# One group of row sums in the last half, a last output block in two column halves, and a new order for every operation

## The chip, the core and the metric

The kernel runs on one core of a Trainium2 chip. TensorE (PE) multiplies matrices, VectorE (DVE), ScalarE (ACT) and GpSimd (POOL) work element by element, and SyncE (SP) issues the DMA transfers. Each engine has its own queue and works it off in order; semaphores make an engine wait for another. The metric is the device time of one execution in microseconds, as the median over several runs.

## What is computed

Two stages follow each other. The first is a retention: per batch and head a 64 x 64 state decays and gathers outer products, and each row of q is multiplied with it.

```python
for t in range(S):                       # S = 768, 4 batches, 8 heads, D = 64
    state = gamma * state + einsum('bhd,bhe->bhde', k[:, :, t], v[:, :, t])
    y[:, :, t] = scale * einsum('bhd,bhde->bhe', q[:, :, t], state)
```

The heads' outputs side by side are x, 4 batches of 768 rows with 512 columns. The second stage is a mixture of four attention experts: two experts are chosen per row by a gate, each has its own q, k, v and output weights with 64 inner columns, and the attention is causal.

```python
logits = x @ w_gate                      # the two largest of 4 experts per row, softmax over the two
for e in range(4):
    q, k, v = x @ wq[e], x @ wk[e], x @ wv[e]
    a = exp(causal(scale * q @ k.T) - max);  a /= a.sum(-1) + 1e-09
    out += w[:, e] * (a @ v @ wo[e])     # w is 0 where e is not chosen
```

## The kernel before

The 768 rows of each batch are two halves of 384 rows (`HS`), so there are eight half-sequences j = 0 to 7; each has three blocks (`CH` = 3) of 128 rows (`C`). The four experts are two pairs p, with two experts e in each.

Retention works on 24 chunks of 128 rows (6 in a batch), each as two steps of 64 rows. For each chunk SP loads `qkT_t` (L245) and `kv_t` (L249), 512 KB each; DVE (first chunk) or POOL multiplies decay factors in (L260 for k, L275 for q); `h2` (L380, L386) computes the part inside the steps and `h1` (L321, L325) the state and its product. ACT and DVE turn the result into `xh` and `xl`, a high and a low part, so that three matmuls in a reduced format replace one in full precision. The weights come in the same way: `wload` (L214) brings a piece into a buffer that is free at the start, ACT (L220) writes its high part and DVE (L221) its low part.

For each half j follow: `proj` (L436, q and k), `vgate` (L478, v and gate logits, per block), `gate` and `gate2` (the two weights per row; `wn` has them per row, `wt` transposed), `mpass` (L559, L573, row maxima on DVE), `mrow` (L602), `score` (L685, L686: transposed scores into `ps`, ACT's exponential L692 into `pt`, a causal select L698 on POOL for diagonal blocks, and additions of all `pt` of a pair into `ac`, L707 and L714, on DVE or POOL) and `av` (L731: `pt` times v, gathered in `ob`, 64 rows for each expert of the pair).

The rows' sums of exponentials divide the result. For j = 0 to 6 this is `norm_a` and `norm_b`: 12 matmuls (L754) of columns of `sel` with `ac` put the sums of all experts and blocks into one tile `f`; DVE adds 1e-9 (L760), takes reciprocals (L764) and multiplies with the expert weights `wt` (L765); SP writes `f` to DRAM (L768) and reads it back spread over partitions (`fe`, L772); POOL multiplies `on`, a copy of `ob`, with `fe` (L781), ACT rounds to `oh` (L783), and POOL subtracts to get `ol` (L786).

For the last half j = 7 there is `norm_last(j, p, c)`, six times, for each pair p and block c. It sums `ac` over partitions with two matmuls against `ones` (f1, L801), copies the block of `ob` with ACT (L806), makes the factors in `rw` in three small DVE steps (f2, L810 to L812), spreads them with two matmuls of `rw` against the identity into `fb` (f3, L818), multiplies on DVE (L822), rounds on ACT (L824) and subtracts on DVE (L827). `wout` (L845) then multiplies `oh` and `ol` with the output weights, three matmuls for each pair, six for each block; ACT evicts 128 x 512 (L853), and SP writes 256 KB (L855).

The order of the work is not that of the code. Each call of `op` records one operation: its engine, a function that emits its instructions, and what it reads and writes. `arrange(ORDER, SLOTS)` at the end emits them in the order of a literal table of operation numbers, and a second table names, for each kind of buffer, which of its few slots each new buffer takes. The framework puts the semaphores in.

## Time and profile before

| | us |
|---|---|
| median of 3 runs | 328.45 (327.85 to 329.1) |
| span of the profiled execution | 325.9 |
| time of that execution beside its span | taken for the median: 2.55 more |

| engine | busy us | share of the span |
|---|---|---|
| PE | 315.4 | 97% |
| DVE | 172.3 | 53% |
| POOL | 169.7 | 52% |
| ACT | 130.1 | 40% |

A profile row gives the start in us, the busy time in us, the engine, the line, the operation, what it writes and reads, the shape, and how many instructions are put together; brackets hold the idle time of the engine before it and what ended it. "x4" for a full-precision matmul of two halves counts the trace's own records, two for each matmul of the program. Matmuls overlap in the pipeline, so the time that one takes of TensorE is the distance to the next one's start, not its busy time.

### The profile page before, as it was taken

The numbers are of one execution on the slowest core, as the hardware profiler recorded it, in microseconds if no ns is written. First come the engines' busy times: TensorE is split into PE (matmuls) and PEld (weight loads), VectorE is DVE, ScalarE is ACT, GpSimd is POOL, SyncE is SP. The second block draws the span as 40 slices with busy tenths as digits, with TensorE's granted clock in tenths as the row PEclk, the third lists the DMA queues.
The fourth block names the chain that finished last, engine by engine and source line by source line (L and its number), as shares of the span: only waits on it lengthen the run. The fifth ranks groups of instructions, "written<-read, shape, count | busy, mean of one in ns | idle before, by whom it ended". The sixth has DMA issues, their size and how long they took to land.

```text
span 325.9 us, 11205 instructions
## 1 busy us (share of the span) xinstructions
PE 315.4 (97%) x4738; PEld 274.7 (84%) x4738; DVE 172.3 (53%) x478; ACT 130.1 (40%) x322; POOL 169.7 (52%) x189
## 2 busy tenths in 40 slices
PE   7599999999999999999999999999999999999995
PEld 3489998898988799979988799989879799887673
DVE  1654566665553354866352453856434234886842
ACT  1244212442734226422636224443433525437633
POOL 6665323561793967333398752671375731922800
PEclk9959999999999999999999999999999999999999
DMA  7994996434746627526646474374320503423022
GB/s 276 384 384 143 249 291 209 152 95 120 198 129 215 230 82 183 142 85 197 179 134 193 166 242 129 80 232 157 98 61 2 165 24 91 134 78 114 0 100 98
DMA packets 22072, 50.82 MB, mean 156 GB/s; under 512 B 3619, under 2 KB 8311, under 8 KB 22021
## 3 DMA queue, kind: packets, MB, share of 16 engines
q1 hardware_dynamic: 22020, 50.10, 49.8%
q8 instruction: 37, 0.61, 0.7%
q14 instruction: 15, 0.11, 0.1%
HBM read 30.71 MB, written 6.79 MB: 115 GB/s over the span
## 4 chain that ended last, share of the span: by engine, by line
PE 94%; DMA 3%; DVE 1%; issue 1%; ACT 1%; SPq 0%; ACTq 0%; DVEq 0%
PE ps L436 21%; PE ps L478 11%; PE ps L845 11%; PE ps_o L731 10%; PE ps L685 7%; PE ps L686 7%; PE ps_st L321 6%; PE ps L386 5%; PE ps L573 4%; PE ps L559 2%; PE ps L325 2%; PE ps L380 2%; PE ps L754 2%; DMA ot<-in_wvg_dram 2%; PE ps_st L731 1%; DMA am_t<-in_amask_dram 1%
## 5 line engine op out<-in xcount | busy, mean ns | idle before, releaser
L692 ACT ACTIVATE pt<-ps 128x384 f32<-128x384 f32 (+2 forms) x112 | 49.1, 493 | 15.8 <-PE ps L686 14.6
L581 DVE CUSTOM_DVE_ANT_0 scr<-ps,cmask_t 128x128 bf16<-128x128 f32 (+3 forms) x64 | 29.8, 487 | 35.3 <-PE ps L573 34.9
L698 POOL TENSOR_SCALAR_AFFINE_SELECT pt<-pt 128x256 f32<-128x256 f32 x48 | 20.9, 445 | 50.1 <-ACT pt L692 39.8
L436 PE MATMUL ps<-xh,qk_hi 128*128 128x384 f32 x128 | 44.0, 344 | 0.0
L685 PE MATMUL ps<-q,k 128*128 128x384 f32 (+2 forms) x144 | 43.9, 318 | 0.0
L436 PE MATMUL ps<-xh,qk_lo 128*128 128x384 f32 x128 | 43.2, 338 | 0.4 <-issue 0.4
L436 PE MATMUL ps<-xl,qk_hi 128*128 128x384 f32 x128 | 43.1, 336 | 0.0
L686 PE MATMUL ps<-q,k 65*128 65x384 f32 (+2 forms) x144 | 42.2, 313 | 0.0
L714 POOL TENSOR_TENSOR ac<-ac,pt 128x256 f32<-128x256 f32 (+2 forms) x32 | 39.9, 1248 | 1.9
L275 POOL TENSOR_TENSOR qd<-qkT_t,qdec_t 128x512 f32<-128x512 f32 (+1 forms) x23 | 27.9, 1212 | 24.7 <-issue 11.0
L707 POOL TENSOR_TENSOR ac<-pt,pt 128x512 f32<-128x512 f32 (+1 forms) x14 | 21.3, 1525 | 32.2 <-ACT pt L692 31.7
L731 PE MATMUL ps_o<-pt,vt 128*64 128x384 f32 (+2 forms) x252 | 35.5, 421 | 0.0
L441 ACT ACTIVATE k<-ps 128x384 fp32r<-128x384 f32 x32 | 15.7, 492 | 49.3 <-PE ps L436 49.3
L335 DVE TENSOR_TENSOR sblk<-ps_st,sdec_t 128x256 f32<-128x256 f32 x44 | 18.5, 421 | 29.7 <-PE ps_st L321 21.7
L348 ACT ACTIVATE xh<-ps 128x512 fp32r<-128x512 f32 x24 | 14.3, 597 | 45.4 <-PE ps L325 45.4
L321 PE MATMUL ps_st<-kv_t 64*64 64x64 f32 x704 | 30.0, 224 | 1.8 <-POOL kv_t L260 0.7
L380 PE MATMUL ps<-am,kv_t 64*64 64x64 f32 x768 | 27.8, 223 | 2.5 <-issue 2.3
L260 POOL TENSOR_TENSOR kv_t<-kv_t,kdec_t 128x512 f32<-128x512 f32 (+1 forms) x23 | 22.4, 977 | 14.8 <-DMA kv_t<-in_kv_dram 11.4
L321 PEld LDWEIGHTS ps_st<-kv_t 64*64 64x64 f32 x704 | 25.1, 137 | 5.9 <-issue 3.6
L731 PEld LDWEIGHTS ps_o<-pt,vt 128*64 128x64 f32 x252 | 16.6, 136 | 15.8 <-issue 11.7
L325 PE MATMUL ps<-qd,sblk 64*64 64x64 f32 x704 | 29.9, 224 | 0.0
L478 PE MATMUL ps<-vg_hi,xh 128*128 128x260 f32 x96 | 28.8, 300 | 0.0
(115 smaller groups left out, 781.5 us busy)
## 6 DMA issues: line engine op xcount, KB each, us to landing
kv_t<-in_kv_dram SPq DMA_DIRECT2D x24, 512.0 KB
qkT_t<-in_qkT_dram SPq DMA_DIRECT2D x24, 512.0 KB
out_dram<-ot SPq DMA_DIRECT2D x24, 256.0 KB
q<-k SPq DMA_DIRECT2D x28, 192.0 KB
k<-q SPq DMA_DIRECT2D x14, 192.0 KB
k<-k SPq DMA_DIRECT2D x14, 192.0 KB
fe<-fd SPq DMA_DIRECT2D x28, 96.0 KB
pt<-in_wqk_dram SPq DMA_DIRECT2D x4, 256.0 KB
```

The source lines that it names most:

```text
L321: nc.tensor.matmul(ST[b].t[rows(rt), s * D:(s + 1) * D], kvs(m, 0, s)[rows(rt)], kvs(m, 1, s)[rows(rt)], start=c == 0 and s == 0, stop=Fal ...
L325: nc.tensor.matmul(yo(m, rt, s), SB[m % 2][rows(rt), s], LD[g, 2].t[rows(rt), s, m % 2 * SC:(m % 2 + 1) * SC], start=m % 2 == 0 and s == 0 ...
L380: nc.tensor.matmul(yo(2 * g + u, rt, s), kvs(u + 2 * g, 1, s)[rows(rt)], amg.t[rows(rt), u, s], start=g % NC == 0 and u == 0 and s == 0, s ...
L436: nc.tensor.matmul(pb.t[:, :HS], ww[:, kt, wsl], xx[:, kt], start=n == 0, stop=n == 11)
L478: nc.tensor.matmul(pb.t[:, :NV + E], xx[:, kt, sl], ww[:, kt], start=n == 0, stop=n == 11)
L581: lambda: nc.vector.tensor_tensor_reduce(scr.t[:, :n1], pb.t[:, :n1], K["cmask"][:, HS + C - n1:], 1.0, mx0.t[:, e, i:i + 1] if prior else ...
L685: nc.tensor.matmul(o, k1.t[:, e, ko:ko + C], q1.t[:, e, q0:], start=True, stop=False)
L686: nc.tensor.matmul(o, k2.t[:65, e, ko:ko + C], q2.t[:65, e, q0:], start=False, stop=True)
L692: lambda es=es, sb=sb, n=n: nc.scalar.activation(pt.t[:, es[0]:es[0] + n, q0:], sb.t[:, :n * w].rearrange("p (e t) -> p e t", e=n), AF.Exp ...
L714: op(eng, cost, lambda: en.tensor_tensor(ac.t[:, :, q0:], ac.t[:, :, q0:], pt.t[:, :, q0:], op=OP.add), r=[(pt, 0), (pt, 1), (ac, "b")], w ...
L731: nc.tensor.matmul(ob.t[e * 64:e * 64 + 64, q0:HS], vt.t[:, ko // C, ee * 64:ee * 64 + 64], pt.t[:, e, q0:], start=kb == 0, stop=kb == las ...
L845: nc.tensor.matmul(wb.t, oo[:, sl], ww[:, p], start=n == 0 and p == 0, stop=n == 2 and p == NP - 1)
```

## The change

First, `norm_f(j)` is split off from `norm_a`: the sums and the three DVE steps that make `f`. The last half runs it once, for all pairs and blocks, so `ones`, `rw`, f1 and f2 go. Its f3 takes a column of the identity, spread to 64 columns, as the stationary operand and `f` as the moving one. ACT now copies `fb` to `on`, and DVE multiplies `ob` with that. The dependency of `ob` is kept per block of 128 columns, so a block is free to be read when its last `av` is through. Second, the last block of `wout` is done in two halves of 256 columns, each with its own `ps`, eviction (part 0 on ACT, part 1 on DVE) and DMA of 128 KB. Third, `stream_a` appends the last half's `norm_last` and `wout` units at its end. Fourth, ORDER and SLOTS are new from the first entry on, for 1549 operations instead of 1555. Line numbers shift by a few: L754 is now L753, L818 is L811, L845 is L842, L853 is L856, L855 is L858.

```diff
--- before.py
+++ after.py
@@ -176,7 +176,6 @@
-    RW = tag("rw", 2, [128, 2])
@@ -231,7 +230,6 @@
-    ones = sbuf.tile([128, 1], F32, name="ones")
@@ -731,20 +729,21 @@
                 nc.tensor.matmul(ob.t[e * 64:e * 64 + 64, q0:HS], vt.t[:, ko // C, ee * 64:ee * 64 + 64],
                                  pt.t[:, e, q0:], start=kb == 0, stop=kb == last, skip_group_check=True)
 
-        op("PE", 3.75 * (HS - q0) * COL, fn, r=[(vt, ko // C), (pt, 0), (pt, 1)], w=[(ob,)],
+        op("PE", 3.75 * (HS - q0) * COL, fn, r=[(vt, ko // C), (pt, 0), (pt, 1)],
+           w=[(ob, c) for c in range(q0 // C, CH)],
            new=[ob] if kb == 0 else [], mode="128x64")
         if kb == last and j < NJ - 1:
             on = ONB[j, p] = Buf(ON)
-            op("ACT", act_c(HS), lambda: nc.scalar.activation(on.t, ob.t[:, :HS], AF.Copy), r=[(ob,)], w=[(on,)],
+            op("ACT", act_c(HS), lambda: nc.scalar.activation(on.t, ob.t[:, :HS], AF.Copy),
+               r=[(ob, c) for c in range(CH)], w=[(on,)],
                new=[on])
 
     def actok(ac):
         return [(ac, "a"), (ac, "b")]
 
-    def norm_a(j):
+    def norm_f(j):
         DONE.add(("n", j))
-        sb, f, fd, fe, wt = Buf(PB), Buf(FF), Buf(FD), Buf(FE), WTB[j // 2]
-        FEB[j] = fe
+        sb, f, wt = Buf(PB), Buf(FF), WTB[j // 2]
         acs = [ACB[j, p] for p in range(NP)]
         c0 = j % 2 * CH
 
@@ -765,6 +764,14 @@
             nc.vector.tensor_tensor(f.t, f.t, wt.t, op=OP.mult)
 
         op("DVE", 1.3, f2, r=[(f,), (wt,)], w=[(f,)])
+        return f
+
+    FLAST = []
+
+    def norm_a(j):
+        f, fd, fe = norm_f(j), Buf(FD), Buf(FE)
+        FEB[j] = fe
+        c0 = j % 2 * CH
         op("SP", 0.4, lambda: nc.sync.dma_start(fd.t, f.t), r=[(f,)], w=[(fd,)], new=[fd], nbytes=65536)
         for e in range(E):
             def bc(e=e):
@@ -788,39 +795,28 @@
 
     def norm_last(j, p, c):
         sl = slice(c * C, c * C + C)
+        if not FLAST:
+            FLAST.append(norm_f(j))
         if c == 0:
             OS[j, p] = (Buf(OH), Buf(OL))
             ONB[j, p] = Buf(ON)
         oh, ol = OS[j, p]
-        on, ac, ob, wnb = ONB[j, p], ACB[j, p], OTB[j, p], WNB[j // 2]
+        on, ob, f = ONB[j, p], OTB[j, p], FLAST[0]
         fresh = c == 0
-        nb, fb, rw = Buf(PB), Buf(PB), Buf(RW)
-
-        def f1():
-            for e in range(2):
-                nc.tensor.matmul(nb.t[:, e:e + 1], ac.t[:, e, sl], ones, start=e == 0, stop=e == 1,
-                                 skip_group_check=True)
-
-        op("PE", 0.4, f1, r=actok(ac) + [("ones",)], w=[(nb,), (rw, "n")], new=[nb, rw],
-           mode="128x128")
-        op("ACT", act_c(C), lambda: nc.scalar.activation(on.t[:, sl], ob.t[:, sl], AF.Copy), r=[(ob,)],
-           w=[(on, c)], new=[on] if fresh else [])
-
-        def f2():
-            nc.vector.tensor_scalar(rw.t, nb.t[:, :2], 1e-9, None, op0=OP.add)
-            nc.vector.reciprocal(rw.t, rw.t)
-            nc.vector.tensor_tensor(rw.t, rw.t, wnb.t[:, 2 * p:2 * p + 2, CH + c], op=OP.mult)
-
-        op("DVE", 0.5, f2, r=[(nb,), (wnb,)], w=[(rw,)])
+        fb = Buf(PB)
 
         def f3():
             for e in range(2):
-                nc.tensor.matmul(fb.t[e * 64:e * 64 + 64, :C], rw.t[:, e:e + 1].to_broadcast([128, 64]), K["ident"],
+                r = (2 * p + e) * 32 + CH + c
+                nc.tensor.matmul(fb.t[e * 64:e * 64 + 64, :C], K["ident"][:, r:r + 1].to_broadcast([128, 64]), f.t,
                                  start=True, stop=True, skip_group_check=True)
 
-        op("PE", 0.24, f3, r=[(rw,), ("ident_t",)], w=[(fb,)], new=[fb], mode="128x64")
-        op("DVE", dve_c(C), lambda: nc.vector.tensor_tensor(on.t[:, sl], on.t[:, sl], fb.t[:, :C], op=OP.mult),
-           r=[(on, c), (fb,)], w=[(on, c)])
+        op("PE", 0.24, f3, r=[(f,), ("ident_t",)], w=[(fb,), (on, c, "n")], new=[fb] + ([on] if fresh else []),
+           mode="128x64")
+        op("ACT", act_c(C), lambda: nc.scalar.activation(on.t[:, sl], fb.t[:, :C], AF.Copy), r=[(fb,)],
+           w=[(on, c)])
+        op("DVE", dve_c(C), lambda: nc.vector.tensor_tensor(on.t[:, sl], ob.t[:, sl], on.t[:, sl], op=OP.mult),
+           r=[(on, c), (ob, c)], w=[(on, c)])
         op("ACT", act_c(C), lambda: nc.scalar.activation(oh.t[:, sl], on.t[:, sl], AF.Copy), r=[(on, c)], w=[(oh, c)],
            new=[oh] if fresh else [])
         op("DVE", dve_c(C),
@@ -829,31 +825,38 @@
 
     WP = {}
 
-    def wout(j, i, pairs=(0, 1)):
+    def wout(j, i, pairs=(0, 1), part=None):
         b, half = divmod(j, 2)
         hi, lo = W["wo"]
         first = pairs[0] == 0
+        n0, n1 = (0, Dm) if part is None else (part * 256, part * 256 + 256)
         if first:
-            WP[i] = Buf(PB)
-        wb = WP[i]
+            WP[i, part] = Buf(PB)
+        wb = WP[i, part]
         sl = slice(i * C, i * C + C)
         os = [OS[j, p] for p in pairs]
 
         def fn():
             for p, (oh, ol) in zip(pairs, os):
                 for n, (oo, ww) in enumerate(((oh.t, hi), (oh.t, lo), (ol.t, hi))):
-                    nc.tensor.matmul(wb.t, oo[:, sl], ww[:, p], start=n == 0 and p == 0, stop=n == 2 and p == NP - 1)
+                    nc.tensor.matmul(wb.t[:, :n1 - n0], oo[:, sl], ww[:, p, n0:n1], start=n == 0 and p == 0,
+                                     stop=n == 2 and p == NP - 1)
 
         last = pairs[-1] == NP - 1
         ot = Buf(OT) if last else None
-        op("PE", 3 * len(pairs) * 0.233, fn, r=[(x, i) for o in os for x in o] + wtok("wo"),
+        op("PE", 3 * len(pairs) * (n1 - n0) * 0.455e-3, fn, r=[(x, i) for o in os for x in o] + wtok("wo"),
            w=[(wb,)] + ([(ot, "n")] if last else []), new=[b for b, y in ((wb, first), (ot, last)) if y],
            mode="128x128")
         if last:
-            op("ACT", act_c(512), lambda: nc.scalar.activation(ot.t, wb.t, AF.Copy), r=[(wb,)], w=[(ot,)])
+            if part == 1:
+                op("DVE", dve_c(256), lambda: nc.vector.tensor_copy(ot.t[:, :256], wb.t[:, :256]), r=[(wb,)],
+                   w=[(ot,)])
+            else:
+                op("ACT", act_c(n1 - n0),
+                   lambda: nc.scalar.activation(ot.t[:, :n1 - n0], wb.t[:, :n1 - n0], AF.Copy), r=[(wb,)], w=[(ot,)])
             r0 = half * HS + i * C
-            op("SP", 0.4, lambda: nc.sync.dma_start(out[b, r0:r0 + C], ot.t), r=[(ot,)], w=[("out", j, i)],
-               nbytes=262144)
+            op("SP", 0.4, lambda: nc.sync.dma_start(out[b, r0:r0 + C, n0:n1], ot.t[:, :n1 - n0]), r=[(ot,)],
+               w=[("out", j, i, part)], nbytes=512 * (n1 - n0))
 
     def wouts(j):
         return [(COST["wout"], lambda i=i: wout(j, i)) for i in range(CH)]
@@ -876,10 +879,6 @@
                     u.append((4 * w(kb - 1) * COL, lambda p=p, kb=kb: av(j, p, kb - 1)))
                     if kb < nkb and kb >= 2 and wl:
                         u.append(wl.pop(0))
-                if j == NJ - 1 and kb > CH:
-                    i = kb - CH - 1
-                    u.append((COST["norm"] / 3, lambda p=p, i=i: norm_last(j, p, i)))
-                    u.append((COST["wout"] / 2, lambda p=p, i=i: wout(j, i, (p,))))
         if j:
             us[0].insert(1, (0, lambda: norm_b(j - 1), ("n", j - 1)))
         if j < NJ - 1:
@@ -891,7 +890,14 @@
             for k in range(NP):
                 u += us[k][:2]
                 us[k] = us[k][2:]
-        return u + wl
+        u += wl
+        for c in range(CH):
+            for p in range(NP):
+                u.append((COST["norm"] / 3, lambda p=p, c=c: norm_last(j, p, c)))
+            for x in range(2 if c == CH - 1 else 1):
+                for p in range(NP):
+                    u.append((COST["wout"] / 2, lambda p=p, c=c, x=x: wout(j, c, (p,), x if c == CH - 1 else None)))
+        return u
 
     def merge(lists, offs=(0, 0, 0)):
         tot = [sum(x[0] for x in l) + 1e-9 for l in lists]
@@ -926,7 +932,6 @@
-        op("DVE", 0.06, lambda: nc.vector.memset(ones, 1.0), w=[("ones",)])
@@ -1006,93 +1011,96 @@
 ORDER = (
...
-    3, 1, 2, 5, 6, 4, 7, 12, 8, 13, 9, 10, 14, 19, 20, 21, 99, 0, 23, 100, 101, 102, 103, 26, 1313, 24, 25, 22, 28,
...
+    0, 22, 3, 1, 23, 4, 25, 27, 5, 98, 28, 2, 24, 14, 56, 7, 6, 26, 9, 12, 13, 44, 58, 37, 39, 40, 38, 43, 48,
...
 SLOTS = {
...
-    "f": "0000000",
+    "f": "00000000",
-    "kv_t": "012012012012012012012012",
+    "kv_t": "012021020122101201010222",
-    "on": "0120120120120120",
-    "ot": "01210210102102102102102102",
+    "on": "0120102102120212",
+    "ot": "012010210122101200121200120",
-    "qd": "010101010101010101010101",
-    "qkT_t": "012012012012012012012012",
-    "rw": "010101",
+    "qd": "010101010101001011010100",
+    "qkT_t": "012012012020221020120120",
...
 }
```

Three places show how the tables move instructions. The first is SP's queue at the start of the program, which loads the chunks (`qkT_t`, `kv_t`), constants (`am_t`, `sdec_t`, `qdec_t`, `kdec_t`) and the v weights (`in_wvg_dram`). Before:

```order
L249 DMA kv_t_66<-in_kv_dram 128x1024
L245 DMA qkT_t_63<-in_qkT_dram 128x1024
L195 DMA am_t<-in_amask_dram 128x256
L195 DMA sdec_t<-in_sdec_dram 128x48
L195 DMA qdec_t<-in_qdec_dram 128x256
L195 DMA kdec_t<-in_kdec_dram 128x48
L245 DMA qkT_t_64<-in_qkT_dram 128x1024
L249 DMA kv_t_67<-in_kv_dram 128x1024
L214 DMA ot_127<-in_wvg_dram 128x260
L245 DMA qkT_t_65<-in_qkT_dram 128x1024
```

After:

```order
L247 DMA kv_t_66<-in_kv_dram 128x1024
L243 DMA qkT_t_63<-in_qkT_dram 128x1024
L194 DMA kdec_t<-in_kdec_dram 128x48
L194 DMA sdec_t<-in_sdec_dram 128x48
L194 DMA am_t<-in_amask_dram 128x256
L247 DMA kv_t_67<-in_kv_dram 128x1024
L243 DMA qkT_t_64<-in_qkT_dram 128x1024
L194 DMA qdec_t<-in_qdec_dram 128x256
L213 DMA ot_127<-in_wvg_dram 128x260
L247 DMA kv_t_68<-in_kv_dram 128x1024
```

The number behind a name is the buffer. `kv_t_67` takes chunk 1 before and chunk 2 after; chunk 1's load of `kv` was the second of its kind, ahead of the first weights, and is now the third (`kv_t_68`), behind the first weights. `qdec_t` stands later, `kdec_t` earlier. The second place is TensorE in the last half, where the last scores are through. `ps_o` and `ps_st` are the `ob` of the two pairs. Before:

```order
L818 MATMUL ps_145<-ident_t,rw_133 64x128 x2
L731 MATMUL ps_o_146<-pt_111,vt_94 64x128 x2
L731 MATMUL ps_st_147<-pt_112,vt_94 64x256 x2
L818 MATMUL ps_142<-ident_t,rw_134 64x128 x2
L801 MATMUL ps_143<-ones,ac_116 128x1 x2
L801 MATMUL ps_141<-ones,ac_117 128x1 x2
L845 MATMUL ps_144<-wo_hi,oh_121 128x512
L845 MATMUL ps_144<-wo_lo,oh_121 128x512
L845 MATMUL ps_144<-wo_hi,ol_123 128x512
L731 MATMUL ps_st_147<-pt_114,vt_94 64x128 x2
L818 MATMUL ps_140<-ident_t,rw_133 64x128 x2
```

After:

```order
L753 MATMUL ps_138<-ac_116,sel 32x128 x2
L753 MATMUL ps_138<-ac_117,sel 32x128 x2
L729 MATMUL ps_st_145<-pt_115,vt_93 64x384 x2
L729 MATMUL ps_st_145<-pt_114,vt_93 64x384 x2
L729 MATMUL ps_st_145<-pt_111,vt_93 64x384 x2
L811 MATMUL ps_142<-f_125,ident_t 64x128 x2
L811 MATMUL ps_143<-f_125,ident_t 64x128 x2
L729 MATMUL ps_st_145<-pt_112,vt_94 64x384 x2
L811 MATMUL ps_139<-f_125,ident_t 64x128 x2
L811 MATMUL ps_141<-f_125,ident_t 64x128 x2
L811 MATMUL ps_140<-f_125,ident_t 64x128 x2
L842 MATMUL ps_138<-wo_hi,oh_121 128x512
```

The sums are one group (L753, of which the last two rows are shown) ahead of the PV steps of the second pair, and the f3 (L811) of both pairs stand together ahead of the first output block. The third place is TensorE's end, the last output block. Before:

```order
L845 MATMUL ps_142<-wo_hi,oh_121 128x512
L845 MATMUL ps_142<-wo_lo,oh_121 128x512
L845 MATMUL ps_142<-wo_hi,ol_123 128x512
L845 MATMUL ps_142<-wo_hi,oh_122 128x512
L845 MATMUL ps_142<-wo_lo,oh_122 128x512
L845 MATMUL ps_142<-wo_hi,ol_124 128x512
```

After:

```order
L842 MATMUL ps_141<-wo_hi,oh_121 128x256
L842 MATMUL ps_141<-wo_lo,oh_121 128x256
L842 MATMUL ps_141<-wo_hi,ol_123 128x256
L842 MATMUL ps_142<-wo_hi,oh_122 128x256
L842 MATMUL ps_142<-wo_lo,oh_122 128x256
L842 MATMUL ps_142<-wo_hi,ol_124 128x256
L842 MATMUL ps_141<-wo_hi,oh_122 128x256
L842 MATMUL ps_141<-wo_lo,oh_122 128x256
L842 MATMUL ps_141<-wo_hi,ol_124 128x256
```

Three matmuls of the second column half (`ps_142`, first pair) stand further up; the second column half is complete first, and the first column half (`ps_141`) last.

More of the change, by code (lines that the diff above doesn't have):

```diff
@@ L1092 @@
     "gs": "0000",
-    "k1": "0123402134201324",
-    "k2": "0123402134201324",
-    "kv_t": "012012012012012012012012",
+    "k1": "0123402314230214",
+    "k2": "0123402314230214",
+    "kv_t": "012021020122101201010222",
     "lg": "0101",
@@ L1103 @@
     "ol": "0101010101010101",
-    "on": "0120120120120120",
-    "ot": "01210210102102102102102102",
+    "on": "0120102102120212",
+    "ot": "012010210122101200121200120",
     "ps": (
-        "0123450123450214352104315204135024150315251340512340152401523150423510431502413052341035412035410235"
-        "4120530241503245132405324102540314034013520143051234051350423502315024531204135021432045301254021543"
-        "0251243025413024530125032513041520301254310243512043125043210451320415203452104320135401253142503142"
-        "5312403512105421305421305241254352041530421350421350214351203451205312035410324510324124530125402531"
-        "405231405231502"
+        "0123450123450214320403124532405412504321042350431504251340253402543154250124501320451345213452134203"
+        "2541453205241302105310430145105234021354023540145032530521341023420153423124150345140324503421503243"
+        "1025301432014520345134053124314015342053241534213052413432152304235401230514231524520143502145302145"
+        "3120532135142053142051235043213415201435201352043510423523402134120531250413205140253410523140254132"
+        "04513204523"
     ),
@@ L1114 @@
     "ps_st": "000000",
-    "pt": "012345021354021354021354021354021354021354021354021354021350214350503214503214",
+    "pt": "012345021341024315023415231450132405125403521304152304025143410532214035154230",
     "q1": "0120120120120120",
     "q2": "0120120120120120",
-    "qd": "010101010101010101010101",
-    "qkT_t": "012012012012012012012012",
-    "rw": "010101",
-    "scr": "011010011010101010101010100110101001101000101010100110101010101010101010101001011001101001010010",
+    "qd": "010101010101001011010100",
+    "qkT_t": "012012012020221020120120",
+    "scr": "010110011010101010010101100111010100010110101010010101001101011010100101010010101110010110101001",
     "vt": "01201201",
```

149 rows, old and new, of the table ORDER are left out of this document.

## The prediction

> **What bounds the kernel now.** I read the engine summary first, then the chain of work that ended last.
>
> ```profile
> PE 315.4 (97%) x4738; PEld 274.7 (84%) x4738; DVE 172.3 (53%) x478; ACT 130.1 (40%) x322; POOL 169.7 (52%) x189
> PE 94%; DMA 3%; DVE 1%; issue 1%; ACT 1%; SPq 0%; ACTq 0%; DVEq 0%
> ```
>
> TensorE is busy for 97% of the span and is 94% of the chain. The other engines are near half. So a microsecond counts only if it is taken from TensorE's own work, from the stretches in which it stands, or from the tail behind its last matmul. The windows view, with PE busy as the first entry after the width and the granted clock behind the engines, says where it stands:
>
> ```profile
> 8.00:16.00 8.00, 4.32 (x222) 3.79 (x222) 5.46 (x9) 1.77 (x5) 5.46 (x5) 1.00 1.03 384
> 16.00:24.00 8.00, 7.44 (x176) 6.87 (x166) 3.91 (x6) 3.38 (x7) 5.26 (x4) 0.57 1.01 387
> 40.00:306.00 266.00, 265.58 (x3871) 233.46 (x3872) 145.08 (x406) 110.09 (x275) 145.00 (x156) 1.00 0.48 142
> 322.00:325.90 3.90, 0.33 (x2) 0.00 (x0) 0.00 (x0) 0.60 (x1) 0.00 (x0) 1.00 0.36 134
> ```
>
> From 40 to 306 us TensorE is idle for 266.00 − 265.58 = 0.42 us. A new order cannot win more than that there; it can only lose. The start is different: 8.00 − 4.32 = 3.68 us idle from 8 to 16 us, with DMA full (1.03, 384 GB/s), and then a clock of 0.57 from 16 to 24 us, which costs 8 × 0.43 = 3.4 us. The tail after the last matmul is 3.57 us. The largest single stop at the start is in the list of waits:
>
> ```profile
> PE ps L380 <- issue: 2.3, 1, 2.3
> ```
>
> Nothing that the profile shows released TensorE there.
>
> **The change, part by part.** *The six column sums go.* Each pair of a block ran two fp32 matmuls of `ac` against `ones` (L801, four trace rows a group). The timeline of TensorE has the distance from each group's start to the start of what follows:
>
> ```profile
> 307.38 0.56 PE L801 MATMUL ps<-ones,ac 128*128 128x1 f32 x4
> 307.79 0.31 PE L685 MATMUL ps<-q,k 128*128 128x128 f32 x1
> 309.72 0.50 PE L801 MATMUL ps<-ones,ac 128*128 128x1 f32 x4
> 310.08 0.48 PE L845 MATMUL ps<-wo_hi,oh 128*128 128x512 f32 x1
> 314.30 1.05 PE L801 MATMUL ps<-ones,ac 128*128 128x1 f32 x8
> 315.21 0.48 PE L845 MATMUL ps<-wo_hi,oh 128*128 128x512 f32 x1
> 316.89 1.05 PE L801 MATMUL ps<-ones,ac 128*128 128x1 f32 x8
> 317.81 0.47 PE L845 MATMUL ps<-wo_hi,oh 128*128 128x512 f32 x1
> ```
>
> 0.41 + 0.36 + 0.91 + 0.92 = 2.60 us for all 24 rows (a row of x8 is two groups). All of it is on TensorE, which is full here, so −2.60.
>
> *One group of sums comes.* It is what the seven halves before already run:
>
> ```profile
> 286.17 0.86 PE L754 MATMUL ps<-ac,sel 128*32 128x128 f32 x24
> 286.96 0.44 PE L573 MATMUL ps<-k,q 128*128 128x384 f32 x1
> ```
>
> 286.96 − 286.17 = +0.79. The f3 matmuls stay six pairs, only with the operands exchanged, so I cost them at nothing.
>
> *The last output block in halves.* Six matmuls of 512 columns become twelve of 256:
>
> ```profile
> 321.70 0.39 PE L845 MATMUL ps<-wo_lo,oh 128*128 128x512 f32 x1
> 321.94 0.40 PE L845 MATMUL ps<-wo_hi,ol 128*128 128x512 f32 x1
> 306.74 0.28 PE L685 MATMUL ps<-q,k 128*128 128x256 f32 x1
> 306.86 0.28 PE L686 MATMUL ps<-q,k 65*128 65x256 f32 x1
> ```
>
> 6 × 0.24 against 12 × 0.12: no difference. Behind the last matmul stand an eviction, an issue on SP and a transfer:
>
> ```profile
> 322.42 0.60 ACT L853 ACTIVATE ot<-ps 128x512 f32<-128x512 f32 x1 [0.80 <-PE ps L845]
> 308.47 0.39 ACT L692 ACTIVATE pt<-ps 128x256 f32<-128x256 f32 x1 [0.42 <-PE ps L686]
> 295.06 0.52 SPq L855 DMA_DIRECT2D out_dram<-ot  x1
> GB/s 0 0 0 0 105 336 336 357 420 378 441 252 63 0 0 0 0 0 0 210 483 357 399 357 378 378 127 0 0 0 0 0 0 0 0 0 0 0 0 0
> ```
>
> (The last line cuts 322 to 325.9 us into 40 slices of 0.0975 us.) A 256-column eviction takes 0.39 instead of 0.60: −0.21. But the other half is ready only 3 × 0.12 = 0.36 us earlier, and its DMA issue holds SP for 0.52, so the last issue comes about 0.2 later than its data: the gain is used up. The last 256 KB fill slices 19 to 26, 0.78 us at some 370 GB/s; half the bytes take 0.4 less. So −0.4; at best both gains (−0.6), at worst none, if the two halves' transfers run into each other (0).
>
> *The start.* SP loads in another order. The last piece of the v weights is the 15th load in both, with the same bytes ahead, and its conversion is where the first v block waits:
>
> ```profile
> 15.87 0.42 ACT L220 ACTIVATE vg_hi<-ac 128x260 fp32r<-128x260 f32 x1 [3.11 <-DMA ac<-in_wvg_dram]
> 9.63 1.04 POOL L260 TENSOR_TENSOR kv_t<-kv_t,kdec_t 128x512 f32<-128x512 f32 x1 [0.36 <-DMA kv_t<-in_kv_dram]
> 18.10 0.58 PE L478 MATMUL ps<-vg_hi,xh 128*128 128x260 f32 x1
> ```
>
> Chunk 1's `kv` now has 0.66 MB more ahead, 1.7 us at the 384 GB/s of this window, so POOL's L260 starts at about 11.35 and ends at 12.4, and TensorE's next states wait about 1.3 us longer. I think that the 2.3 us stop that comes next takes most of this, because the late weights come last either way: +0.1. Upper bound, all of it is passed on: +1.3. Lower bound, the stop does not recur and the v block starts as soon as its weights are there (15.87 + 0.42 = 16.29 instead of 18.10): −1.8.
>
> *The new waits at the end.* Sums of both pairs now wait for all ten additions into `ac` on DVE, and all of f waits on DVE before the first f3:
>
> ```profile
> L760 DVE TENSOR_SCALAR f<-ps 128x128 f32<-128x128 f32 x7 | 2.0, 285 | 3.4 <-ACT k L441 2.8 <-PE ps L754 0.6
> L764 DVE RECIPROCAL f<-f 128x128 f32<-128x128 f32 x7 | 6.7, 951 | 0.2
> L765 DVE TENSOR_TENSOR f<-f,wt 128x128 f32<-128x128 f32 x7 | 2.0, 292 | 0.2
> 302.59 0.87 PE L731 MATMUL ps_o<-pt,vt 128*64 128x384 f32 x4
> 303.29 2.75 PE L731 MATMUL ps_st<-pt,vt 128*64 128x384 f32 x16
> ```
>
> 0.285 + 0.951 + 0.292 = 1.53 us. Under it the new order puts three PV steps; one (four rows) takes 303.29 − 302.59 = 0.70, so 2.1 us. That covers it with 0.6 over for the semaphores; without the cover it would cost all 1.5. The chain f3, ACT copy, DVE product, ACT `oh`, DVE `ol` behind it is five short steps under one PV step and three f3, with a few tenths over. Adding what can slip here: +0.3, between 0 and +1.
>
> *Everything between* is rearranged and I cost it at 0: the most it can win is the 0.42 us of idle time above, and what it can lose is the rivals' matter.
>
> **The sum**, against the profiled execution: 325.9 − 2.60 + 0.79 − 0.4 + 0.1 + 0.3 = 324.1 us of span. The median before lies 328.45 − 325.9 = 2.55 above this span, so 324.1 + 2.55 gives **326.6 us**. With the terms' likely errors, this case runs from 325.4 to 327.8.
>
> **The rivals.** *A: the start comes out faster.* The 0.57 clock from 16 to 24 us follows the half-empty window ahead of it. If the new order stops TensorE less, the clock may not fall: up to 3.4 us more, 326.6 − 3.4 = 323.2. For it: chunk 1's states are moved next to the stop. Against it: the loads run at 384 GB/s all through, and the new order puts nothing into that window that does not wait for them. [...]
>
> *B: the gain is eaten at the end by DVE and POOL.* The additions on DVE, the norm products of half 6 on POOL and the causal selects on POOL now stand close together, and they slow each other:
>
> ```profile
> 296.09 0.95 DVE L707 TENSOR_TENSOR ac<-pt,pt 128x768 f32<-128x768 f32 x1
> 302.51 1.80 DVE L707 TENSOR_TENSOR ac<-pt,pt 128x768 f32<-128x768 f32 x1 [0.85 <-ACT pt L692]
> 302.49 1.00 POOL L786 TENSOR_TENSOR ol<-on,oh 128x384 fp32r<-128x384 f32 x1
> 299.46 0.41 POOL L698 TENSOR_SCALAR_AFFINE_SELECT pt<-pt 128x256 f32<-128x256 f32 x1 [8.87 <-ACT pt L692]
> 299.84 2.69 POOL L781 TENSOR_TENSOR on<-on,fe 128x384 f32<-128x384 f32 x2
> ```
>
> The same addition takes 0.95 alone and 1.80 when a POOL operation of 1.00 started just before. Between the last score and the sums there are now only the three output blocks of half 6, 18 × 0.24 = 4.3 us, under which the last exponentials, a select and the last additions must pass. Two collisions in that chain cost 2 × 0.85 = 1.7, less the few tenths of slack: about +1.3, so 327.9, the same time as before. The selects of the last pair also queue behind the two L781 products, which wait for a DMA of f. For B: the additions cannot be spread any more, since one group reads all. Against: half of this stood there already, with TensorE 16.00 of 16 us busy. [...]
>
> *C: slower, through the chunk loads.* Chunk 11's `qkT` is now the eighth that is loaded, ahead of chunk 7's, and sits in one of three buffers until it is used, so chunks 7 to 10 share two. By the new order only about 6.6 us of TensorE work, at the durations of this trace, lie between the release of the buffer for chunk 7 and its use (12.6 before). In it must pass an issue on SP (0.52), the transfer of 512 KB (1.4 us at 384 GB/s, 2.6 at 200) with its completion (the last output took 1.3 us from its last byte to the end of the span), and POOL's product:
>
> ```profile
> L275 POOL TENSOR_TENSOR qd<-qkT_t,qdec_t 128x512 f32<-128x512 f32 (+1 forms) x23 | 27.9, 1212 | 24.7 <-issue 11.0 <-PE ps L325 10.9 <-DMA qkT_t<-in_qkT_dram 2.8
> ```
>
> 0.5 + 0.8 + 2.6 + 1.3 + 1.2 = 6.4 us (0.8 from the end of the last eviction to its first bytes). If SP or POOL has one more operation ahead of it, about 1 us each time, TensorE stops for about 1 us in each of four chunks: 326.6 + 4 = 330.6. It decides as soon as the loads come about 1 us later than this. Against it: the loads are asked for in an order that a queue of SP carries out without other big transfers at that place.
>
> **Chances.** Forecast 0.50, A 0.10, B 0.25, C 0.15. A measurement of this kernel can tell about 0.5%, 1.64 us: faster is below 326.8, slower above 330.1. The forecast lies just below the first bound, so of its 0.50 I give 0.33 to faster and 0.17 to the same; A is faster; of B 0.05 faster and 0.20 the same; of C 0.02 the same and 0.13 slower. Faster 0.48, same 0.39, slower 0.13. The range reaches from 324.3, which leaves out most of A, to 329.2, which holds B and leaves out C.
>
> **What the new profile would show.** Right: no single-column sums at the end, one group of 24 rows of 0.8 us, TensorE idle below 1 us from 40 to 306 us and almost none from 306 to the last matmul, the last matmul about 1.5 us earlier, a tail of 3.2 instead of 3.57 us. A: a clock above 0.57 from 16 to 24 us. B: a wait of TensorE on DVE's additions at the sums, or on a select at a PV step of the last half. C: TensorE waiting on `qd` where chunks 7 to 10 are read. Wrong would be above all a first stretch that ends more than 1 us later, or middle idle time above 1.5 us.

## The result, and the profile after

| | before | changed |
|---|---|---|
| median, us | 329.11 (326.62 to 329.61, 10 runs) | 329.93 (328.35 to 332.99, 10 runs) |
| ratio to before | | 1.0061 (95% interval 1.0034 to 1.0089) |
| span of the profiled execution | 325.9 | 331.3 |

The ratio says slower by 0.6%, where the forecast was faster; the two medians lie 0.25% apart, and a second ten executions (e11 below) gave 1.0024 (0.9987 to 1.0060). So the forecast gain is absent, and the loss is small. Some executions come out over 1.5% above the fastest of their kernel; the ratios leave these out, and where the profile fell on one the table of the experiments gives no span. The profiled execution of the changed kernel is the slowest of its ten (332.99 us); the other nine have spans from 326.6 to 329.9. Time and span differ by 1.7 us here, not by 2.55: the one execution profiled before was a quick one, and the prediction took its distance to the median for a constant.

The page of the changed kernel, the rows that answer to those of before:

```profile
PE 316.1 (95%) x4744; PEld 273.4 (83%) x4744; DVE 173.2 (52%) x463; ACT 130.0 (39%) x322; POOL 169.6 (51%) x189
PE 86%; DMA 7%; issue 2%; SPq 2%; DVE 1%; ACT 1%; DVEq 0%; ACTq 0%
```

TensorE's busy time is the same, its share of the chain fell from 94% to 86%, and DMA has 7% instead of 3%. The windows (PE busy behind the width, the granted clock behind the five engines):

```profile
8.00:16.00 8.00, 4.24 (x232) 3.69 (x227) 3.49 (x7) 1.27 (x4) 4.30 (x4) 1.00 0.99 342
16.00:24.00 8.00, 6.84 (x153) 6.34 (x154) 5.78 (x11) 4.41 (x9) 6.68 (x6) 0.79 0.82 277
40.00:306.00 266.00, 260.52 (x3825) 229.43 (x3825) 142.12 (x397) 106.15 (x266) 144.99 (x160) 0.99 0.48 140
```

From 40 to 306 us TensorE is idle for 5.48 us where it was idle for 0.42. In two later profiles of the same kernel (e11, e15) it is 3.03 and 2.99 us. TensorE's waits name the three largest pieces in this one:

```profile
PE ps L684 <- DMA q<-md: 2.1, 1, 2.1
...
PE ps_st L319 <- issue: 1.4, 2, 1.3
...
PE ps L378 <- issue: 1.3, 1, 1.3
```

The first is at 205 us, where a score step waits for the row maxima (`md` and a row of `q`, by way of DRAM). The other two are at 42 and 48 us, with nothing that the profile shows ahead of them. The end of the program, in TensorE's and DVE's timelines:

```profile
317.02 0.86 PE L753 MATMUL ps<-ac,sel 128*32 128x128 f32 x24
319.80 0.61 PE L811 MATMUL ps<-f,ident_t 128*64 128x128 f32 x8
...
324.63 0.44 PE L729 MATMUL ps_st<-pt,vt 128*64 128x128 f32 x4 [0.18 <-DVE on L818]
```

```profile
314.53 2.48 DVE L712 TENSOR_TENSOR ac<-ac,pt 128x768 f32<-128x768 f32 x3 [0.30 <-POOL pt L696]
317.95 0.29 DVE L759 TENSOR_SCALAR f<-ps 128x128 f32<-128x128 f32 x1 [0.95 <-PE ps L753]
318.28 0.95 DVE L763 RECIPROCAL f<-f 128x128 f32<-128x128 f32 x1
```

The additions end at 317.01 and the sums start at 317.02: this wait is tight but costs at most a tenth. f is ready at 319.56, f3 starts at 319.80 without a wait. The one wait shown is 0.18 us. Behind the last matmul 3.37 us are left instead of 3.57.

### Where the late row maxima come from

SP's timeline of the changed kernel ahead of the 2.1 us wait:

```profile
192.10 0.34 SPq L858 DMA_DIRECT2D out_dram<-ot  x1
192.56 0.36 SPq L247 DMA_DIRECT2D kv_t<-in_kv_dram  x1
193.03 0.38 SPq L243 DMA_DIRECT2D qkT_t<-in_qkT_dram  x1
...
194.21 0.34 SPq L243 DMA_DIRECT2D qkT_t<-in_qkT_dram  x1
194.65 0.38 SPq L775 DMA_DIRECT2D fd<-f  x1
201.16 1.11 SPq L779 DMA_DIRECT2D fe<-fd  x2
202.36 0.43 SPq L611 DMA_DIRECT2D md<-mt  x1
...
204.32 0.24 SPq L613 DMA_DIRECT2D q<-md  x1
```

and the chain of waits over the same stretch:

```profile
194.65 6.49 DMA fd<-f
...
202.36 1.90 DMA md<-mt
...
204.32 3.24 DMA q<-md
```

In 2.1 us SP issues an output (256 KB) and three chunk loads (512 KB each), 1.8 MB, and right behind them the 64 KB of `f`. The write of `f` lands 6.49 us after its issue. SP stands at the read-back `fe`, which needs them, and behind it in the same queue stand `md` and `q<-md`, which have nothing to do with `f`. Before, the two loads ahead of that write were issued more than 3 us earlier, and its read-back was not reached before 200 us:

```profile
190.95 0.33 SPq L245 DMA_DIRECT2D qkT_t<-in_qkT_dram  x1
191.38 1.72 SPq L249 DMA_DIRECT2D kv_t<-in_kv_dram  x1
194.43 0.33 SPq L768 DMA_DIRECT2D fd<-f  x1
...
200.36 1.19 SPq L772 DMA_DIRECT2D fe<-fd  x2
```

A slower stretch follows the stop. TensorE's timeline (a matmul of 384 columns takes 0.34 at full clock):

```profile
207.60 0.44 PE L684 MATMUL ps<-q,k 65*128 65x384 f32 x1 [2.11 <-DMA q<-md]
...
209.09 0.52 PE L434 MATMUL ps<-xh,qk_lo 128*128 128x384 f32 x1
...
211.88 0.34 PE L434 MATMUL ps<-xh,qk_lo 128*128 128x384 f32 x1
```

From 208.4 to 211.8 us, 3.4 us, the granted clock is 0.50 and each step takes 0.32 instead of 0.175; the stop ahead of it was 2.1 us long. The slow stretch does not come behind every such stop: it stands behind one of 1.7 us in e11 (clock 0.96 from 185 to 225 us) and one of 2.6 us in e13 (0.99 from 185 to 225 us, 0.98 from 225 to 300), but it did not come in e2, e14 and e15, where TensorE stood for about 2 us as well (clock 1.00 from 185 to 225 us). What sets it off is not shown.

### The profile page after: what moved, and what is told of

The parts are those of the page before. It is cut to its first block, busy times and chain, and to the rows that moved or that the text cites. A ratio compares the mean times of both kernels' runs of the same rounds, so it can differ in the third digit from the quotient of the medians.

```text
span 331.3 us, 11204 instructions
## 1 busy us (share of the span) xinstructions
PE 316.1 (95%) x4744; PEld 273.4 (83%) x4744; DVE 173.2 (52%) x463; ACT 130.0 (39%) x322; POOL 169.6 (51%) x189
## 4 chain that ended last, share of the span: by engine, by line
PE 86%; DMA 7%; issue 2%; SPq 2%; DVE 1%; ACT 1%; DVEq 0%; ACTq 0%
PE ps L434 20%; PE ps L842 10%; PE ps_o L729 10%; PE ps L476 10%; PE ps L683 6%; PE ps L684 6%; PE ps_st L319 5%; PE ps L384 4%; PE ps L571 4%; PE ps L378 2%; DMA fd<-f 2%; PE ps L557 2%; DMA qdec_t<-in_qdec_dram 2%; PE ps L323 2%; PE ps L753 2%
## 5 line engine op out<-in xcount | busy, mean ns | idle before, releaser
L690 ACT ACTIVATE pt<-ps 128x384 f32<-128x384 f32 (+2 forms) x112 | 50.0, 493 | 20.5 <-PE ps L684 17.9
L696 POOL TENSOR_SCALAR_AFFINE_SELECT pt<-pt 128x256 f32<-128x256 f32 x48 | 20.5, 439 | 57.6 <-ACT pt L690 41.8
L684 PE MATMUL ps<-q,k 65*128 65x384 f32 (+2 forms) x144 | 43.0, 313 | 2.1 <-DMA q<-md 2.1
L434 PE MATMUL ps<-xh,qk_hi 128*128 128x384 f32 x128 | 44.6, 348 | 0.0
L434 PE MATMUL ps<-xh,qk_lo 128*128 128x384 f32 x128 | 43.8, 342 | 0.0
L434 PE MATMUL ps<-xl,qk_hi 128*128 128x384 f32 x128 | 43.7, 341 | 0.0
L683 PE MATMUL ps<-q,k 128*128 128x384 f32 (+2 forms) x144 | 43.2, 317 | 0.0
L712 POOL TENSOR_TENSOR ac<-ac,pt 128x256 f32<-128x256 f32 (+2 forms) x32 | 39.9, 1248 | 1.7
L729 PE MATMUL ps_o<-pt,vt 128*64 128x384 f32 (+2 forms) x252 | 36.5, 423 | 0.0
L384 PE MATMUL ps<-qkT_t 64*64 64x64 f32 x768 | 28.4, 220 | 1.8 <-DMA qkT_t<-in_qkT_dram 1.3
L476 PE MATMUL ps<-vg_hi,xh 128*128 128x260 f32 x96 | 28.4, 295 | 1.7 <-ACT vg_hi L219 1.7
L684 PEld LDWEIGHTS ps<-q,k 65*128 65x128 f32 x144 | 27.4, 190 | 2.5 <-DMA q<-md 2.4
```

The lines of the kernel that those rows point to most:

```text
L384: nc.tensor.matmul(ps.t[rows(rt), a:a + SC], qb.t[rows(rt), 1, s, t], qb.t[rows(rt), 0, s, t], start=True, stop=True)
L434: nc.tensor.matmul(pb.t[:, :HS], ww[:, kt, wsl], xx[:, kt], start=n == 0, stop=n == 11)
L476: nc.tensor.matmul(pb.t[:, :NV + E], xx[:, kt, sl], ww[:, kt], start=n == 0, stop=n == 11)
L683: nc.tensor.matmul(o, k1.t[:, e, ko:ko + C], q1.t[:, e, q0:], start=True, stop=False)
L684: nc.tensor.matmul(o, k2.t[:65, e, ko:ko + C], q2.t[:65, e, q0:], start=False, stop=True)
L690: lambda es=es, sb=sb, n=n: nc.scalar.activation(pt.t[:, es[0]:es[0] + n, q0:], sb.t[:, :n * w].rearrange("p (e t) -> p e t", e=n), AF.Exp ...
```

## The experiments

Ratios are to the kernel before, on the same chip.

| kernel | ratio (95% interval) | span of its profile, us |
|---|---|---|
| e1 tail only | 0.9949 (0.9920 to 0.9978) | 323.7 |
| e5 tail only, whole last block | 0.9954 (0.9925 to 0.9984) | 324.3 |
| e2 order only | 1.0100 (1.0053 to 1.0147) | 329.3 |
| e11 changed, again | 1.0024 (0.9987 to 1.0060) | 328.2 |
| e15 changed, third profile | | 327.2 |
| e3, e13, e14 two loads moved | 1.0020 (0.9988 to 1.0051) | 326.5, 329.1, 328.6 |
| e16 loads in order | 1.0020 (0.9983 to 1.0056) | 327.4 |
| e4 start of before | 1.0133 (1.0081 to 1.0184) | 332.5 |
| e8 start to 56 us and tail | 1.0007 (0.9976 to 1.0038) | 328.6 |
| e9 start to 77 us and tail | 0.9988 (0.9952 to 1.0023) | 327.5 |
| e12 start to 21 us and tail | 0.9951 (0.9924 to 0.9979) | |
| e10 middle, two loads moved | 1.0040 (1.0001 to 1.0078) | 328.7 |
| e6 shifted instructions | 1.0229 (1.0153 to 1.0306) | |
| e7 two loads moved and shifted | 1.0165 (1.0118 to 1.0211) | 332.4 |

### The end alone, and the order alone (e1, e2, e5)

Both tables are orders of nearly the same operations, so they can be cut and joined where they have emitted nearly the same set. They are joined at 266 us of before (274 of the changed kernel).

```diff
 ORDER = (
-    <the changed kernel's entries up to 274 us>
+    <the entries of before up to 266 us, in the changed kernel's numbers>
     <the rest in the changed kernel's order>
```

> The order of before up to 266 us, then the changed last half (one sums group, last block in halves) in its new order. Theory 1: the new end is worth what its segment shows (274.2 us to the end of the span 331.3 is 57.1 us, where before took 266.2 to 325.9, 59.7 us: 2.6 us less) and the loss lies wholly in the new order ahead of it, so this runs at about 326.5 us where before runs at 329.1, ratio 0.992. Rival: the end gains nothing by itself (the gain is eaten by additions and POOL), ratio 1.000 within 0.003.

> The kernel before, its own last half with six column sums and a whole last block, but ahead of it (up to 274 us) the new order. Theory 1: slower than before by what the new order loses, 2.6 us for the end's gain and 2 us for the measured difference, 3.5 to 5 us, ratio 1.011 to 1.015. Rival (the end lost it): ratio 1.000 within 0.003.

The tail alone is faster by 0.51%, 1.7 us of 328, less than the 2.6 expected. The new order alone, with the old tail, is slower by 1.0%, 3.3 us. Their product, 0.9949 × 1.0100 = 1.0048, lies between the two series of the changed kernel, 1.0061 and 1.0024: the parts add up, and rival B, the gain eaten at the end, falls. e5 takes the last block's halves back:

```diff
-            for x in range(2 if c == CH - 1 else 1):
+            for x in range(1):
-                    ... wout(j, c, (p,), x if c == CH - 1 else None)
+                    ... wout(j, c, (p,))
```

> The tail-only kernel (order of before up to 266 us, changed end) with the last output block whole again: 512 columns, one eviction on ACT, one DMA of 256 KB. Tail-only measured a ratio to before of 0.9949. Theory: of those 1.7 us the one sums group carries 1.4 and the shorter drain (3.37 instead of 3.57 us behind the last matmul) 0.2 to 0.4, so 0.9955 to 0.996 here. Rival: the halves carry most of it, ratio 0.998 or more.

0.9954 against 0.9949: the halves are worth 0.05%, which this cannot tell from nothing. What is left, the one group of sums and the new order of the last half, carries the gain; no run takes these two apart.

### The loads ahead of f (e3, e11, e13, e14, e15, e16)

```diff
 SP, near 193 us
     out_dram<-ot
-    kv_t<-in_kv (chunk 22)
     qkT_t<-in_qkT (chunk 20)
-    qkT_t<-in_qkT (chunk 21)
     fd<-f;  fe<-fd x2;  md<-mt;  kv_t<-in_kv (chunk 21);  q<-md
+    qkT_t<-in_qkT (chunk 21)
+    kv_t<-in_kv (chunk 22)
     kv_t<-in_kv (chunk 19)
```

> The changed kernel with two of the 512 KB chunk loads (kv of chunk 22, qkT of chunk 21) moved on SP's queue from ahead of the write of f to behind the row-max transfers of half 4. Theory 1a: TensorE's 2.1 us wait for the row maxima at 205 us comes from f's 64 KB write standing behind 1.8 MB of other transfers (6.5 us to land), with the row-max transfers behind it on SP; with two loads moved (1 MB, 2.7 us at 384 GB/s) it goes, and with it the halved clock that follows: 2 to 3.5 us less than the changed kernel in an execution that has it, so about 327 us, ratio to before 0.993 to 0.997. Rival: the wait was one slow DMA of that execution; then no difference from the changed kernel, ratio 1.006.

In e3's profile the write of f lands in 3.5 us and the stop is gone. TensorE's window from 185 to 225 us, in turn for the changed kernel, e11 and e3 (before: 40.00 busy of 40):

```profile
185.00:225.00 40.00, 37.89 (x649) 33.76 (x640) 20.57 (x53) 12.84 (x34) 17.18 (x20) 0.96 0.56 164
```

```profile
185.00:225.00 40.00, 38.30 (x613) 33.90 (x613) 23.61 (x53) 13.48 (x36) 17.74 (x23) 0.96 0.56 173
```

```profile
185.00:225.00 40.00, 40.00 (x710) 34.99 (x707) 22.11 (x61) 14.37 (x37) 20.89 (x25) 1.00 0.59 173
```

Idle time plus lowered clock is 2.1 + 1.6 = 3.7 us in the first profile of the changed kernel and 1.7 + 1.6 = 3.3 in the second. The second (e11) shows the other branch of the same chain:

> The changed kernel once more, for a second profile. Theory 1a: the write of f lands 6 to 6.5 us after its issue again and the row maxima are late by 1 to 2 us at 205 us. Theory 2: if the stops at matmul 858 and 985 are a matter of the single execution, they can be absent or of another length; where TensorE stops without a releaser it is at 221 plus a multiple of 127 or 128 matmuls.

```profile
191.65 5.57 DMA fd<-f
...
197.75 2.78 DMA fe<-fd
...
200.66 1.02 POOL on L788
201.71 0.52 ACT oh L790
202.23 0.39 ACT k L439
...
202.64 0.56 DVE q L442
```

Here the maxima were nearly in time, but POOL, ACT and DVE were held up one behind the other by `fe`, and TensorE lost its time at 209 us waiting for DVE. In all five profiles that issue the three loads ahead of f (the changed kernel's three, e2, e4) f took 5.6 to 6.5 us.

And yet e3's times are not clearly better than the changed kernel's: 1.0020 (0.9988 to 1.0051), where 0.993 to 0.997 was expected, against 1.0061 and 1.0024. Three more profiles were taken for that.

> A second profile of the changed kernel with the two chunk loads moved. In its first one the stop near 200 us was gone, but the two fetch stops at matmul 858 and 985 (3.1 us together) were there. If these are a matter of the single execution, this profile has a chance of a span near 323.5 us without them; if they belong to this program, they are here again.

> A third profile of the same kernel, for the same question: with two of three or three of three showing both stops, they belong to this program; with one of three, to the execution.

> A third profile of the changed kernel: its first had both fetch stops (span 331.3), its second none (328.2). The loss between 185 and 215 us, 3.5 to 4 us in both, should be here for the third time; the stops are open.

e15 repeats the loss (37.77 busy of 40 us at full clock, 2.2 us). In e13 and e14 the stop at 205 us is gone as in e3, the fetch stops of 42 and 48 us are absent, and there is a new wait near 220 us. e13's chain and its wait:

```profile
211.26 10.73 DMA kv_t<-in_kv_dram
...
222.13 1.05 POOL kv_t L258
```

```profile
PE ps_st L319 <- POOL kv_t L258: 4.3, 3, 2.6
```

This is chunk 20's `kv`. The new order loads `kv` in the order 22, 21, 19, 20 (e13 and e14: 21, 22, 19, 20), so chunks 22 and 21 hold two of the three buffers, chunk 20 must wait until chunk 19 has given back the third, and its load has little time. Rival C's mechanism, with `kv` instead of `qkT`, took 2.0 to 2.6 us in two of three profiles once the stop ahead of it was out of the way. e16 puts these four loads in the order of the chunks too.

```diff
 SP, near 200 us and after
-    kv_t (chunk 21) ... kv_t (chunk 22), kv_t (chunk 19) ... kv_t (chunk 20)
+    kv_t (chunk 19) ... kv_t (chunk 20), kv_t (chunk 21) ... kv_t (chunk 22)
```

> The changed kernel with qkT of chunk 21 behind the row-max transfers as in e3, and the kv loads of chunks 19 to 22 in the order of the chunks, so that chunk 22's does not take a buffer early and chunk 20's not the last one. Theory: e3's gain was given back by chunk 20's kv, which in two of three looks landed 10.7 us after its issue and held TensorE for 2.0 to 2.6 us near 220 us; with the loads in order neither the late row maxima at 205 us nor this wait is there, and the kernel has the tail's gain: ratio 0.993 to 0.997. Rival: the loss between 185 and 225 us has another cause and takes a new place, ratio 1.001 or more.

```profile
185.00:225.00 40.00, 39.33 (x704) 34.55 (x703) 21.07 (x60) 13.93 (x36) 20.34 (x24) 1.00 0.60 173
```

In its profile both waits are gone and 0.7 us of idle time are left there. But the ratio is 1.0020 (0.9983 to 1.0056), the rival's outcome as far as the time goes. So the place and the mechanism of these waits are shown by the profiles; that they carry the timed loss, and that the chain's 2 to 3.7 us would come back as time, is not shown.

### The start (e4, e8, e9, e12) and the middle (e10)

Each joins the two orders at another place: e4 has before up to 53 us and then the changed kernel; e8, e9 and e12 have the new order up to 56, 77 and 21 us, then before up to 266 us, then the changed end; e10 has before up to 76 us, then the new middle with e3's loads, then the changed end.

> The changed kernel with the order of before up to 53 us, and with it the chunk loads of qkT in the order of the chunks. Theory 1b: the new start costs 1.7 us by 50 us (two stops of 1.3 us without a releaser at 42 and 48 us), so this is about 1.5 us faster than the changed kernel, ratio to before about 1.001. Rival: the start costs nothing in most executions, and ratio stays at 1.006.

> The new order up to 56 us, then the order of before up to 266 us, then the changed end. Theory 1 (the loss sits at 190 to 215 us and in the two fetch stops at 42 and 48 us): no late row maxima at 200 us, the two stops stay, ratio 0.995 plus 0 to 0.006. Rival: the loss is spread over the whole middle of the new order and its start is better by 1 us: ratio 0.992.

> As the start-and-tail kernel, but with the seam at 76 us, where ten operations differ between the two orders instead of fourteen: the new order up to 77 us, then that of before up to 266 us, then the changed end. The seam at 53 us had cost a wait of 3.3 us for a copied q. Theory: the new start is neutral to 1 us better (lag of 15.2 against 13.5 us in the changed kernel, but 12.3 in the order-only kernel), so ratio 0.992 to 1.000. Rival: the start costs 2 us through its two instruction stops, ratio 1.001 or more.

> The new order only up to 21 us, then that of before up to 266 us, then the changed end. The changed kernel's two profiles reach the work of 15 us (about 25 us of time) 1.0 to 1.2 us earlier than the kernel before. Theory: that adds to the tail's gain, ratio 0.9949 minus 0.003, 0.990 to 0.993. Rival: the lead is given back at the next loads, ratio 0.995 as with the tail only.

> The order of before up to 76 us, then the new order with the two chunk loads moved behind the row-max transfers, then the changed end. What is left of the new order is its middle without the burst of loads. Theory: the burst was the middle's main loss, and 0.5 to 1.5 us stay (three stops of 0.3 to 0.9 us at 114, 134 and 149 us), so ratio 0.9949 plus 0.002 to 0.005. Rival: the middle loses by much more than the burst, ratio 1.002 or more.

e8 and e9 are spoilt by their seams: waits of 3.1 us (at 62 us) and of 1.5 us (at 81 us) on copies between q and k that neither order has there by itself. e4's wait of 1.9 us on DVE is not of this kind: it is the matmul at which e11 waits for 1.7 us, the burst's other branch. e4 joins the 2.0 us stop of before, at 15 us, to the new order's burst, and it was slower than the changed kernel where 1.5 us less was expected. e12 has the ratio of the tail alone, 0.9951, so the start up to 21 us is neutral, though the changed kernel's profiles are a microsecond ahead there. e10 says that the new middle costs without the burst as well: 1.0040 against the tail's 0.9949, 3 us; of the 3.96 us that TensorE is idle in its profile between 40 and 306 us, 1.8 are stops of the kind of the next section and 1.8 are waits for copies between q and k (at 170 and 213 us) that the changed kernel's profiles do not have there. In all three profiles of the changed kernel 0.6 us are idle between 60 and 185 us, where before and e1 have none; 0.2 to 0.4 of it is one stop of the next section's kind.

The middle also costs where TensorE is not idle. A PV step of 384 columns took 0.70 us to the next one (the prediction's rows). In front of a matmul of another tile shape it takes 0.79:

```profile
93.18 0.87 PE L729 MATMUL ps_o<-pt,vt 128*64 128x384 f32 x4
93.97 0.27 PE L319 MATMUL ps_st<-kv_t 64*64 64x64 f32 x1
```

The changed kernel leaves the PV steps eight times ahead of such a matmul behind 384 columns, 0.42 us from the last row's start to the next matmul's, where e1 does it once; behind 128 columns it is 0.20. Added up from start to start without idle time, the same 288 PV rows take 39.9, 40.3 and 39.9 us in the three profiles of the changed kernel, 39.9 in e2, e3 and e16 and 39.8 in e10, but 38.7 in before and 38.8 in e1 and e12. These 1.1 us are in every profile of the new middle, and no wait shows them. No run undoes them by themselves.

### The stops without a releaser (e6, e7)

```diff
         def warm():
-            for i in range(12):
+            for i in range(10):
                 nc.tensor.matmul(pbs[i % 6].t, wu, ...512 columns...)
+            for i in range(90):
+                r = slice(i % 2 * 64, i % 2 * 64 + 64)
+                nc.tensor.matmul(pbs[i % 6].t[r, :64], wu[r, :64], wu[r, :64], start=True, stop=True)
```

> The changed kernel with the same order; only the warm-up at the start is 10 matmuls of 512 columns and 90 small ones of 64 instead of 12 of 512 (78 more matmul and weight-load pairs, about the same time). It leaves nothing of the result out. Theory 2: the stops of 1.5 us at matmul 858 and 985 of the changed kernel are waits for a 16 KB block of instructions (TensorE went on 1.4 us after the block's packet ended, in every stop seen), so with the instructions shifted by 156 the boundaries fall on other matmuls and both stops go from the retention steps at 42 and 48 us, or move; up to 3 us less ahead of 60 us, ratio to before about 1.000. Rival: the stops belong to these steps (data or DVE late), and stay on matmul 858 and 985 counted without the added ones. The 2 to 3.5 us stop near 205 us stays under both.

> The changed kernel with the two chunk loads moved behind the row-max transfers, and with the shifted instructions. If both causes are right and add up: the tail's 1.7 us are left as a gain and about 1 us of the earlier start, ratio to before 0.990 to 0.995. If the fetch stops only move to other dense steps: ratio as with the moved loads alone, 1.002.

The order of the work is untouched, and the kernels become slower by 1.7% (e6 against the changed kernel) and 1.4% (e7 against e3). The edit adds 88 matmuls, 10 and 90 for 12; the expectation's 78 is a slip. The stops of e6 stayed at the same count of matmuls, 858 and 986, which is now other work (88 matmuls earlier in the order), and new ones came at 222, 349 and 1112. Counted so, nearly all stops without a releaser lie on one grid: 221 and 984 in before, e1 and e4, 858 and 985 in the changed kernel and e3, and 222, 349 and 986 in e7, all multiples of about 127.3 apart. Off it are stops of 0.6 to 0.7 us at 156 (e1, e4, e10), 284 (before) and 244 (e7); at these counts other profiles name POOL's work on a load as the releaser, so they are likely such waits. On the grid TensorE went on about 1.4 us (1.3 to 1.6) after a 16 KB packet of the instruction queue had ended: in the changed kernel packets from 41.10 and 46.01 us, 1.09 and 1.85 us long, and TensorE's rows

```profile
43.58 0.27 PE L378 MATMUL ps<-am,kv_t 64*64 64x64 f32 x1 [1.31 <-issue]
...
49.24 0.21 PE L319 MATMUL ps_st<-kv_t 64*64 64x64 f32 x1 [1.27 <-issue]
```

In before it is 13.14 and then 14.54 us (the 2.3 us stop of the prediction). e7's longest, and its waits:

```profile
19.59 0.21 PE L323 MATMUL ps<-qd,sblk 64*64 64x64 f32 x1 [3.44 <-issue]
```

```profile
PE ps L323 <- issue: 5.5, 3, 3.4
```

The longest are in the 64 x 64 retention steps, of which 68 matmuls start in a microsecond (40.8 to 41.8 us of the changed kernel); stops of up to 1.1 us (L434 in e4) stand elsewhere too (L434, L476 and L753). The size of the packets agrees with the grid: in the changed kernel's profile the queue brings 37 of them, 0.61 MB in all, for 4744 matmuls and as many weight loads, which is 128 matmuls a packet beside the 127.3 between the stops. Most packets have no stop of TensorE behind them, and a stop cost up to 3.4 us (e7). Whether a packet shows is a matter of the execution as well: of the 37, the changed kernel's first profile shows four stops (span 331.3, with those at 42 and 48 us), and the other two show one each (328.2 and 327.2).

## Why the prediction was wrong

**The end: right.** Sums and last block were to give −2.60 + 0.79 − 0.4 + 0.3 = −1.9 us. e1 measures −0.51% of 328.2, −1.7 (−0.7 to −2.6). The group of sums took its 0.8 us, and the chain of f stayed under the three PV steps. The drain's −0.4 was too large a size: the profiles show 0.2 (3.37 against 3.57 us), and e5 cannot tell even that from nothing. The waits' +0.3 is 0.2 on DVE's product and at most 0.1 at the sums. That the parts hit so closely is better than e1's interval can tell.

**The start: about right on average by luck, wrong in its reasons.** It was costed at +0.1 between −1.8 and +1.3. The 2.3 us stop was read as something that absorbs lateness; it stands at a fixed count of matmuls, 221, 1.4 us behind the end of an instruction packet (13.14 to 14.54 us), and it does not come in the changed kernel's profiles. There TensorE stands for loads instead: 1.2 to 2.0 us for a `qkT`, 1.4 to 1.5 for chunk 1's `kv` (0.7 before), and 0.5 to 2.0 for the v weights. By 60 us TensorE is idle for 8.73, 6.18 and 5.66 us in the three profiles of the changed kernel, 6.92 in that of before.

**"Everything between is rearranged and I cost it at 0" is the step that failed.** The upper bound was read from idle time, 0.42 us, and the loss was left to rival C alone. e2 puts the cost of the order ahead of the end at 3.3 us, twice the gain. C had the right family of causes, chunk loads and buffers held early, but looked at `qkT` of chunks 7 to 10, where no wait came. What came was at chunks 19 to 22: three loads in a burst ahead of a small write on which the same queue then waits, 2.1 to 2.2 us of TensorE's time from 185 to 225 us in two profiles of the changed kernel and 1.7 in the third. Beside it stand the 1.1 us of the PV steps, which no idle time shows. The prediction's own sign of being wrong, middle idle time above 1.5 us, is there in all three profiles (5.48, 3.03 and 2.99 us). The order tables show this burst, since SP's rows are listed there; I compared that queue at the start and not over its length.

**A and B** did not come. The clock from 16 to 24 us was 0.79 instead of 0.57 in the first two profiles, as A had it, without a gain in the time; in the third it was 0.68 from 8 to 24 us. So the slow stretch of the start changes between executions of one kernel. B's collisions of DVE and POOL did not hold up the sums.

**The offset of 2.55 us** from span to median came from one quick execution; with 1.7 the same forecast would have been 325.8, further off.

**Open:** with the burst and the `kv` order undone (e16) the profile loses little there, but the timed ratio is 1.0020 and not the tail's 0.9949. Against e1's profile that of e16 is 3.7 us longer. By 60 us TensorE is idle for 8.58 us where it is 5.84 in e1, though at a clock of 0.97 against 0.94, which is worth 1.8; from 60 to 225 us it is idle for 1.3 where e1 has none; and the PV steps take 1.1 more. That is 3.3 of the 3.7 us of these two profiles. How much of it lasts over many executions was not measured: in three profiles of one kernel the idle time by 60 us went from 5.66 to 8.73.
